# A fused mLSTM and feed-forward kernel: one list of steps in another order for the opening and the first 21 blocks, weight pieces without a maximum step, output gates in one run per partition

## The chip, the core and the metric

The kernel runs on one core of a Trainium2 chip. A core has a matmul engine (TensorE, here PE, with its weight loads shown apart as PEld), three engines for elementwise work (VectorE or DVE, ScalarE or ACT, GpSimd or POOL), and SyncE (SP), on whose queue this kernel puts all of its transfers. Each engine works through its own queue in order, and the engines wait for one another on semaphores. The metric is the device time of one execution in microseconds (us); lower is better.

## The reference

Four batches of 8 heads, 768 steps, head size 40, go through a gated recurrence with a running maximum m; the result, 3,072 tokens of 320 values, goes through a feed-forward layer with 2,048 hidden values.

```python
for t in range(S):
    m_new = np.maximum(f_gate[:, :, t] + m, i_gate[:, :, t])
    f_stab = np.exp(f_gate[:, :, t] + m - m_new)
    i_stab = np.exp(i_gate[:, :, t] - m_new)
    C = f_stab * C + i_stab * outer(vt, kt)
    n = f_stab * n + i_stab * kt
    h_tilde = C @ qt
    denom = np.maximum(np.abs(n @ qt), 1.0)
    y[:, :, t] = sigmoid(o_gate[:, :, t]) * h_tilde / denom
h = x @ w_in                     # x is y, as 3072 x 320
g = where(h >= 1, h, where(h <= -1, 0, (h + 1) ** 2 / 4))
out = g @ w_out
```

The weights come as 64-bit floats and are made into 32-bit ones in the kernel.

## The kernel before

The recurrence is cut into chunks of 128 steps: 6 chunks of 4 batches are 24 blocks n, four to a chunk. In a block the scores (k times q, one product per head) are multiplied by a matrix of decays and multiplied with the values; from the second chunk on, the state carried over the earlier chunks is added. Four blocks' results, turned, make one 512-token tile j of the feed-forward layer, which runs over 16 column blocks of 128: x = 16 j + block numbers them, 96 in all.

Every engine gets its instructions in the order of one list written out by hand, step by step; the class InOrder (line 102) keeps each engine to that order. There are two such lists. STEPS (line 37) is the opening: the gates' sums, the first four blocks, the first weight piece. ORDER (line 43) is all the rest. A step is a letter and a number. Those that matter here:

- loads on SP: Lg gates of chunk 0, Li the identity for transposes, Lq or Q the q/k tile of a block (two transfers of 160 KB), Lv2 values for two blocks, V values and keys of a block (from block 4 also q), P output gates of a chunk, L or Lw a weight piece (768 or 640 KB), A decays read back, Lf and Lc gates of chunks 1 to 4 and a mask
- PE: E in STEPS (Eb in the new list) the causal mask of a block's decays, A (Ab) the sums picked out of one tile, p (fs) a transpose of those sums, s or C scores, u or U product with the values, t or T the transposes of the result, K state product, I product with the carried state, M and N the two feed-forward products of a block x, J and j a score step with part of a feed-forward product
- elementwise: x or D the exponentials of the decays (ACT), m or c scores times decays (DVE), v or E values times gates (POOL), z s y (in STEPS r f y) the normalizer, the gate product and the result (DVE), x and w (in STEPS z) the high and low part of the turned result (ACT and DVE), Z the sigmoid of a chunk's output gates (ACT), R q r the hidden activation (ACT, ACT, DVE), B1 to B9 the gates of chunks 1 to 4 in a batch (B2 and B4 on DVE, B5 on POOL, B6 transposes on PE), k the state's mask
- the weight pieces: a digit 1 to 7 and the piece's place in the load order; 1 magnitude (ACT), 2 sign (DVE), 3 low half (POOL), 4 maximum (DVE), 5 the assembled word (DVE), 6 its high part (ACT), 7 its low part (DVE). Piece 0 is c, e and d in STEPS. Pieces go in turn to w_in and w_out; M needs a w_in piece for two blocks x, N a w_out piece. Raw pieces have two buffers (wraw)
- heating: wK in STEPS sets a count; the next PE step that calls hot() (line 495) first runs so many matmuls of zeros, 512 columns each, which no result uses

Product M of a block has eight matmuls of 512 columns: four with the high part of x, then two with its low part (made by w), then two more. From block x = 16 on the hidden values are split too (G and g).

load_og (line 510) fetches a chunk's output gates into the one buffer "sig". Its input has 1,280 bytes in a row for each step and batch. word_steps (line 411) and convert (line 437) make the weights.

Of the kernel before, what the change touches and what calls it, by code (L numbers as in the profile page):

```python
# [23 lines left out]
P = 128  # L24
# [12 lines left out]
STEPS = (  # L37
# [3 lines left out]
)  # L41
# [16 lines left out]
M24 u10 E11 A13 A12 r23 z10 G23 N21 R24 s10 y9 q24 y10 M25 r24 i11 G24 S13 g23 T9 R25 g24 N22 x9 S12 q25 w9 X9 D13.0
r25 K10 N23 k10 v11 V12 a10 G25 D12.0 g25 J11.26 N24 D12.1 c11.0 c11.1 U11 K11 u11 E12 N25 z11 V13 v12 k11 A14 s11 T10
p12 P3 M26 x10 y11 l12 D13.1 w10 X10 a11 T11 M27 x11 R26 w11 X11 q26 I12 R27 r26 I13 S14 q27 i12 M28.1 i13 G26 r27 e12  # L60
D14.0 g26 e13 j12.28 G27 M29 c12.0 Q13 R28 g27 Q14 q28 c12.1 Z3 N26 r28 m12 M30 b12 G28 N27 R29 g28 q29 K12 R30 r29
N28 v13 V14 q30 k12 G29 a12 M31 g29 r30 G30 N29 R31 g30 q31 M32 r31 G31 g31 I14 R32 M33 e14 q32 D14.1 r32 U12 G32 M34
# [36 lines left out]
TINY = 2.0  # L99
# [30 lines left out]
def mlstm_ffn_kernel(ctx, tc, qk, qn, vk, og, fi0, fi, fic, w_in, w_out, cst, out):  # L130
# [160 lines left out]
    def gate_exps(c):  # L291
        ex = exs.pop(c)
        tp = psum_a()[:, :P]
# [117 lines left out]
    def word_steps(k, w, raw, eng):  # L411
# [3 lines left out]
        if k > 1 and k != 4:  # L415
# [21 lines left out]
    def convert(k, nw, eng=nc.vector):  # L437
# [538 lines left out]
```

## Time and profile before

| | us |
|---|---|
| median of 3 runs | 486.82 |
| lowest and highest run | 486.24, 493.91 |
| span of the profiled execution | 496.1 |
| PE busy in it | 484.0 |
| DVE busy | 340.6 |
| ACT busy | 289.5 |
| POOL busy | 154.0 |

The profiled execution is one execution, with a span of its own. Its views show, for each engine, when each group of instructions began, how long it took, and what ended the idle time before it. PEclk is the granted clock of TensorE as a share of full speed: 1.00 is 2.4 GHz, 0.50 is 1.2 GHz.

### The profile page before, as it was taken

The numbers are of one execution on the slowest core, as the hardware profiler recorded it, in microseconds if no ns is written. First come the engines' busy times: TensorE is split into PE (matmuls) and PEld (weight loads), VectorE is DVE, ScalarE is ACT, GpSimd is POOL, SyncE is SP. The second block draws the span as 40 slices with busy tenths as digits, with TensorE's granted clock in tenths as the row PEclk, the third lists the DMA queues.
The fourth block names the chain that finished last, engine by engine and source line by source line (L and its number), as shares of the span: only waits on it lengthen the run. The fifth ranks groups of instructions, "written<-read, shape, count | busy, mean of one in ns | idle before, by whom it ended". The sixth has DMA issues, their size and how long they took to land.

```text
span 496.1 us, 8843 instructions
## 1 busy us (share of the span) xinstructions
PE 484.0 (98%) x3403; PEld 414.3 (84%) x3407; DVE 340.6 (69%) x598; ACT 289.5 (58%) x559; POOL 154.0 (31%) x175
## 2 busy tenths in 40 slices
PE   7998999999999999999998999999999999999997
PEld 3785787778779898989897988998989988988896
DVE  5548989899998968668667766948745577453332
ACT  4425786647756557674655954545765376275552
POOL 2503956564815514213324320313301142000000
PEclk8569899999999999999999999999999999999999
DMA  8935685754433215104433122202421100010001
GB/s 231 303 135 165 244 177 190 262 191 157 144 106 112 85 44 180 53 1 131 147 112 122 44 70 82 101 26 79 140 80 58 55 32 1 0 55 0 1 0 54
DMA packets 27737, 51.69 MB, mean 104 GB/s; under 512 B 8312, under 2 KB 17968, under 8 KB 27696
## 3 DMA queue, kind: packets, MB, share of 16 engines
q1 hardware_dynamic: 27696, 51.14, 32.2%
q8 instruction: 27, 0.44, 0.4%
q14 instruction: 14, 0.11, 0.1%
HBM read 47.09 MB, written 4.03 MB: 103 GB/s over the span
## 4 chain that ended last, share of the span: by engine, by line
PE 92%; DVE 3%; DMA 2%; ACT 1%; issue 1%; SPq 1%
PE pso L116 39%; PE psh L116 35%; PE psa L116 18%; DMA raw<-in_qk 1%; DMA qn<-in_qn 1%; DVE z L116 1%; ACT r L116 1%; SPq L116 0%; DVE wl L116 0%; DVE ow L116 0%; DVE sz L116 0%; DVE hv L116 0%; DVE r L116 0%; ACT sig L116 0%; DVE y L116 0%
## 5 line engine op out<-in xcount | busy, mean ns | idle before, releaser
L116 ACT ACTIVATE r<-psh,half 128x512 f32<-128x512 f32 x96 | 65.9, 687 | 90.5 <-PE psh L116 90.0
L116 PE MATMUL psh<-xh,wh 128*128 128x512 f32 x288 | 103.8, 415 | 1.2 <-DVE r L116 1.0
L116 DVE SCALAR_TENSOR_TENSOR r<-psh,r 128x512 f32<-128x512 f32 x96 | 65.8, 687 | 54.0 <-ACT r L116 53.2
L116 PE MATMUL pso<-oh,gh 128*128 128x320 f32 x320 | 101.9, 319 | 0.0
L116 PE MATMUL pso<-ow,gh 128*128 128x320 f32 x320 | 99.0, 309 | 0.0
L116 PE MATMUL pso<-oh,gl 128*128 128x320 f32 x320 | 98.9, 309 | 0.0
L116 PE MATMUL psh<-xh,wl 128*128 128x512 f32 (+1 forms) x274 | 94.7, 403 | 0.1
L116 DVE TENSOR_TENSOR gl<-r,gh 128x512 fp32r<-128x512 f32 x80 | 62.2, 786 | 27.7 <-ACT gh L116 27.5
L116 ACT CAST gh<-r 128x512 fp32r<-128x512 f32 x80 | 48.7, 617 | 46.5 <-DVE r L116 26.8
L116 PEld LDWEIGHTS pso<-oh,gh 128*128 128x128 f32 x320 | 60.2, 188 | 3.3 <-issue 0.7
L116 PEld LDWEIGHTS psh<-xh,wl 128*128 128x128 f32 (+1 forms) x274 | 51.6, 189 | 12.9 <-DVE wl L116 1.1
L116 ACT ACTIVATE r<-r 128x512 f32<-128x512 f32 x96 | 60.7, 632 | 2.7
L116 PEld LDWEIGHTS pso<-ow,gh 128*128 128x128 f32 x320 | 60.3, 188 | 1.9
L116 PE MATMUL psh<-xl,wh 128*128 128x512 f32 x192 | 61.0, 399 | 0.0
L116 PEld LDWEIGHTS pso<-oh,gl 128*128 128x128 f32 x320 | 60.1, 188 | 0.0
L116 PEld LDWEIGHTS psh<-xh,wh 128*128 128x128 f32 x288 | 49.2, 189 | 9.5 <-DVE r L116 1.5
L116 POOL TENSOR_TENSOR v<-vk,G 128x328 f32<-128x328 f32 x36 | 28.8, 801 | 80.1 <-PE psa L116 61.8
L116 ACT ACTIVATE Abc<-Abc,nA 128x128 f32<-128x128 f32 x160 | 50.1, 390 | 0.3 <-POOL Abc L116 0.2
L116 PEld LDWEIGHTS psh<-xl,wh 128*128 128x128 f32 x192 | 36.4, 190 | 8.8
L116 POOL TENSOR_TENSOR m<-m 128x1024 bf16<-128x1024 f32 x12 | 22.9, 1908 | 57.1 <-DVE m L116 57.1
L116 DVE TENSOR_TENSOR Abc<-psa,Abc 128x512 f32<-128x512 f32 x41 | 26.8, 685 | 18.1 <-PE psa L116 13.6
L116 PE MATMUL pso<-ow,r 128*128 128x320 f32 x128 | 37.6, 438 | 0.7 <-DVE ow L116 0.7
(178 smaller groups left out, 712.8 us busy)
## 6 DMA issues: line engine op xcount, KB each, us to landing
Abc<-a_d SPq DMA_DIRECT2D x20, 512.0 KB
raw<-in_qk SPq DMA_DIRECT2D x48, 160.0 KB
vk<-in_vk SPq DMA_DIRECT2D x20, 324.0 KB
wraw<-in_w_in SPq DMA_DIRECT2D x8, 768.0 KB
wraw<-in_w_out SPq DMA_DIRECT2D x8, 640.0 KB
sig<-in_og SPq DMA_DIRECT2D x6, 640.0 KB
qn<-in_qn SPq DMA_DIRECT2D x20, 180.0 KB
out<-o SPq DMA_DIRECT2D x22, 160.0 KB
```

The costliest lines, as they stand in the source:

```text
L116: r = getattr(self.engine, name)(*args, **kwargs)
```

## The change

STEPS and its loop go; the opening is the head of ORDER, with names of its own for what only the opening does (Lg, Li, Lf, Lc, Lv, Eb, Ab, fg, fs, ht, F). Four or fewer letters of a step can now be followed by "+K", the count of heating matmuls. The list is in another order up to step R24; behind that it is unchanged. Step 4 is gone from every weight piece, and step 1 scales by 2^-112 instead of 65,536, so that a zero stays zero. The output gates are laid out by the host as one run of 5,120 bytes per partition and chunk. The opening's block keeps the values' product in PSUM from values_mm itself. Two places more can run heating matmuls (gate_exps and batch_turn).

```diff
-STEPS = (
-    "Lg Li Lo Lq0 Lv0 Lq1 Lw0 Lq2 Lf Lv2 Lq3 Lw1 Lc o w9 E0 g0 q0 p A0 k0 x00 w2 s0 x01 m00 w1 E1 A1 h0 v0 x10 m01 "
-    "w2 s1 x11 v1 Lr0 Lr1 m10 c Lw2 w2 u0 m11 w2 E2 A2 x20 B0 w2 s2 r0 f0 y0 x21 v2 m20 m21 w2 u1 E3 A3 w1 t0 x30 e "
-    "w2 s3 v3 Lr2 Lr3 r1 f1 y1 x31 z0 m30 m31 w2 u2 t1 r2 f2 y2 w2 u3 z1 t2 r3 f3 y3 w8 z2 t3 W3 d z3 "
-)
 ORDER = """
-V4 Q4 Q5 P1 V5 M0 21 11 B1 22 Z1 41 M1 31 B2 B4 B5 51 L3 R0 B3 q0 61 r0 R1 71 32 B6 q1 M2 12 r1 v1 B7 42 L4 v0 52 K1
-v2 A4 R2 K0 A5 23 v4 A6 N0 q2 B8 k0 13 v3 r2 62 33 43 M3 k1 24 E4 L5 53 K2 34 R3 I4 k2 63 S4 N1 i4 q3 73 14 r3 S5 D4.1
...
+Lg fg1 fg2 P0 Z0 ht+7 L0 20 30 Li Eb0+7 fs Ab0 Eb1+3 D0.1 D0.0 10 Ab1 Q0 Lf Lv0 fg3 fg4 Q1 Lv2 E0 C0+1 Eb2+5 D1.0 B0
+50 D1.1 Ab2 D2.1 c0.0 Eb3+2 c0.1 C1 U0 c1.0 Ab3 c1.1 60 B1 z0 Q2 Q3 70 C2 E2 E1 D2.0 c2.0 D3.1 Q4 E3 B2 V0 s0 D3.0
+c2.1 U1 V1 z1 y0 s1 v1 C3+1 c3.1 U2+1 V2 c3.0 U3+3 y1 T0 z2 s2 z3 L1 T1+2 B3 y2 T2 v0 s3 y3 x0 x2 w0 K0 w2 x1 w1 T3 x3
+v2 w3 11 Lc K1 M0 V4 21 F R0 31 k0 B4 V3 B5 K2 k1 51 q0 M1 k2 61 v3 I4 L2 R1 r0 q1 71 22 32 r1 B6 A4 B7 i4 M2 12 52 M3
+K3 R2 L3 23 v4 k3 A5 R3 33 13 53 K4 q2 N0 L4 E4 63 q3 N1 r2 S4 D4.0 73 M4 D4.1 k4 r3 24 V5 M5 L5 14 C4 34 54 25 R5 V6
+15 35 B8 c4.1 P1 v5 55 R4 L6 S5 q4 r4 Q5 D5.1 N2 65 16 c4.0 75 26 L7 36 A6 D5.0 B9 q5 L8 N3 Z1 U4 u4 z4 L10 r5 t4 n4
...
-            nc.scalar.activation(w["mg"], hi.bitcast(F32), AF.Abs, scale=65536.0)
+            nc.scalar.activation(w["mg"], hi.bitcast(F32), AF.Abs, scale=2.0 ** -112)
...
-        elif k == 4:
-            eng.tensor_scalar_max(w["mg"], w["mg"], TINY)
...
-        nc.sync.dma_start(t, og.rearrange("(b c p) e -> c p b e", c=NC, p=P)[c])
+        nc.sync.dma_start(t.rearrange("p b e -> p (b e)"), og[c])
...
+    steps.update({
+        "Lg": first_gates, "Li": lambda: nc.sync.dma_start(ident, cst[:, :P]), "Lf": batch_loads,
+        "Lc": lambda: nc.sync.dma_start(cs_t, cst[0:120, P:]), "Lv": load_v2, "Eb": exponents, "Ab": add_sums,
+        "fg": first_gate_steps, "fs": first_sums, "ht": lambda: hot(psum_a()), "F": end_front,
+    })
     for what in ORDER.split():
-        steps[what[0]](*map(int, what[1:].split(".")))
+        what, _, n = what.partition("+")
+        heat = int(n or 0)
+        name = what.rstrip("0123456789.") or what[0]
+        steps[name](*map(int, filter(None, what[len(name):].split("."))))
...
-    a["og"] = nat(o_gate)
+    a["og"] = nat(o_gate).reshape(B, NC, P, DM).transpose(1, 2, 0, 3).reshape(NC, P, B * DM)
```

In the new list fg1 to fg4 are the first chunk's gates in four parts (running sums; their rests; the tail; a transpose on PE and the exponentials on ACT), and B0 is the batch's maxima, B in STEPS.

## Rows read from the trace of the kernel before

**Rows 1.** The page's busy time by engine: us, share of the span, instructions

```profile
PE 484.0 (98%) x3403; PEld 414.3 (84%) x3407; DVE 340.6 (69%) x598; ACT 289.5 (58%) x559; POOL 154.0 (31%) x175
```

**Rows 2.** Busy time by stretch: start:end, length, engines, PEclk, DMA share, GB/s

```profile
7.00:9.00 2.00, 0.65 (x5) 0.33 (x4) 1.21 (x6) 1.98 (x2) 0.39 (x2) 1.00 1.05 294
...
9.50:32.90 23.40, 22.71 (x123) 17.50 (x122) 10.53 (x21) 8.61 (x31) 6.47 (x10) 0.50 0.85 267
...
42.50:46.50 4.00, 3.99 (x16) 2.90 (x16) 3.87 (x10) 1.90 (x3) 1.70 (x2) 1.00 0.99 323
46.50:49.80 3.30, 0.89 (x5) 0.49 (x5) 1.59 (x3) 3.27 (x5) 2.99 (x6) 1.00 0.48 186
49.80:53.20 3.40, 3.30 (x7) 2.09 (x8) 3.22 (x4) 3.34 (x5) 3.20 (x4) 0.53 0.13 21
...
77.80:78.80 1.00, 0.26 (x2) 0.05 (x1) 1.00 (x2) 0.72 (x2) 0.36 (x2) 1.00 0.84 338
78.80:200.00 121.20, 121.20 (x853) 101.29 (x854) 106.30 (x176) 78.70 (x153) 59.52 (x60) 1.00 0.42 140
```

**Rows 3.** PE in time: start, us, operation, count, idle before and its releaser

```profile
8.96 2.04 PE L116 MATMUL pso<-raw 40*128 40x128 f32 x14 [0.74 <-DMA raw<-in_qk]
...
33.39 1.16 PE L116 MATMUL pso<-raw 40*128 40x128 f32 x16
34.48 0.39 PE L116 MATMUL pso<-zeros 128*128 128x512 bf16 x1
...
37.42 1.87 PE L116 MATMUL psa<-ow,A 128*128 128x41 f32 x16
39.12 0.53 PE L116 MATMUL psa<-ident,y 128*128 128x128 f32 x3
39.49 1.89 PE L116 MATMUL psh<-zeros 128*128 128x512 bf16 x8
...
42.50 0.71 PE L116 MATMUL psh<-xh,wh 128*128 128x512 f32 x2
...
47.64 0.33 PE L116 MATMUL psa<-ident,fi_s 128*128 128x128 f32 x1 [1.16 <-POOL fi_s L116]
49.01 0.33 PE L116 MATMUL psa<-ident,fi_s 128*128 128x128 f32 x1 [1.04 <-POOL fi_s L116]
...
58.82 0.79 PE L116 MATMUL psa<-ow 128*120 128x123 f32 x6
...
78.75 2.42 PE L116 MATMUL pso<-ow,r 128*128 128x320 f32 x8 [0.74 <-DVE ow L116]
```

**Rows 4.** The chain that ended last, 36 to 60 us: start, us, what

```profile
40.49 0.40 SPq L116
...
41.48 4.90 DMA qn<-in_qn
...
57.12 1.87 PE psh L116 x8
```

**Rows 5.** Busy time by stretch again, for the transfers at the start

```profile
0.00:5.00 5.00, 3.71 (x9) 1.34 (x10) 1.94 (x8) 1.28 (x1) 1.97 (x12) 1.00 0.57 150
...
0.00:10.00 10.00, 7.36 (x34) 3.52 (x36) 4.95 (x19) 4.56 (x6) 3.11 (x15) 0.95 0.79 214
```

**Rows 6.** Single rows in time of ACT, DVE and POOL, as in rows 3

```profile
13.68 2.17 ACT L116 ACTIVATE Abc<-pso,nA 128x128 f32<-128x128 f32 x8
...
40.91 0.41 DVE L116 TENSOR_TENSOR xl<-psa,xh 128x256 fp32r<-128x256 f32 x1
41.33 0.29 DVE L116 TENSOR_TENSOR xh<-psa,xh 64x128 fp32r<-64x128 f32 x1
...
46.57 1.02 POOL L116 TENSOR_TENSOR fi_s<-fi_s,ah_u 128x128 f32<-128x128 f32 x1 [1.95 <-DVE ah_u L116]
```

**Rows 7.** DVE by line and form, 40 to 200 us: busy, mean ns

```profile
L116 DVE TENSOR_SCALAR mg<-mg 128x640 f32<-128x640 f32 x8 | 6.7, 838 | 0.0
...
L116 DVE TENSOR_SCALAR mg<-mg 128x768 f32<-128x768 f32 x7 | 4.7, 664 | 0.0
```

More of the change, by code (lines that the diff above doesn't have):

```diff
@@ L58 @@
[L58 to L62, printed above, removed]
@@ new lines @@
+R14 214 M15 314 x7 S9 r12 q14 r13 514 N12 N13 i8 614 r14 w7 I9 72 215 K8 D9.1 M16 315 115 515 N14 i9 74 M17 X5 R15 X7
+76 p8 78 q15 r15 R16 a7 D8.0 612 C8 q16 k8 615 710 712 r16 N15 P2 c8.1 D10.1 M18.1 R17 c8.0 e9 O0.0 G16 O0.1 D10.0
+o0.1 q17 m8 b8 o0.0 J9.18 D9.0 g16 R18 l8 r17 G17 M19 Q10 U8 N16 c9.0 c9.1 O0.2 q18 r18 R19 e8 M20.1 O0.3 m9 b9 q19
+714 E9 j10.20 r19 u8 g17 G18 Z2 N17 Q12 p9 z8 l9 M21 R20 q20 c10.1 G19 v9 c10.0 A11 U9 s8 a8 v10 y8 K9 E10 M22 o0.2
+r20 o0.3 V11 I10 715 R21 q21 k9 u9 r21 T8 x8 G20 z9 g18 R22 Q11 M23 A12 N18 R23 g19 p10 l10 m10 G21 i10 w8 g20 q22 q23
@@ new lines @@
+r22 N19 G22 b10 a9 I11 e11 S11 e10 A13 U10 g22 N20 g21 E11 s9 r23 M24 u10 D11.1 D11.0 z10 N21 G23 X8 R24 s10 y9 q24
+y10 M25 r24 i11 G24 S13 g23 T9 R25 g24 N22 x9 S12 q25 w9 X9 D13.0 r25 K10 N23 k10 v11 V12 a10 G25 D12.0 g25 J11.26 N24
+D12.1 c11.0 c11.1 U11 K11 u11 E12 N25 z11 V13 v12 k11 A14 s11 T10 p12 P3 M26 x10 y11 l12 D13.1 w10 X10 a11 T11 M27 x11
+R26 w11 X11 q26 I12 R27 r26 I13 S14 q27 i12 M28.1 i13 G26 r27 e12 D14.0 g26 e13 j12.28 G27 M29 c12.0 Q13 R28 g27 Q14
+q28 c12.1 Z3 N26 r28 m12 M30 b12 G28 N27 R29 g28 q29 K12 R30 r29 N28 v13 V14 q30 k12 G29 a12 M31 g29 r30 G30 N29 R31
@@ new lines @@
+N38 u14 E15 G40 z14 G39 V17 D16.0 g40 J15.42 g39 M42 G41 s14 Q17 c15.1 A17 c15.0 N39 R42 g41 q42 y14 a15 U15 r42 T14
+u15 E16 A18 M43 x14 z15 S17 w14 X14 s15 I16 R43 y15 P4 M44 e16 q43 i16 D17.1 r43 p16 S18 T15 M45.1 x15 R44 w15 X15 l16
+q44 J16.45 R45 r44 q45 N40 c16.0 Q18 Z4 r45 c16.1 M46 m16 N41 b16 G43 G42 g43 M47 G44 g42 D18.0 g44 N42 R46 q46 U16
+R47 r46 q47 N43 u16 E17 A19 D18.1 r47 z16 M48 p17 G46 s16 l17 G47 g46 D17.0 N44 g47 S19 R48 M49.1 q48 G45 r48 D19.1
+g45 j17.49 M50 c17.0 Q20 R49 c17.1 q49 m17 N45 R50 q50 r49 b17 r50 K16 M51 k16 V18 v17 N46 R51 q51 r51 M52 G48 a16 g48
@@ new lines @@
+N47 R52 q52 M53 r52 O2.3 O2.1 o2.3 G49 o2.1 G51 g49 I17 M54.1 e17 g51 R53 i17 q53 O2.0 D19.0 J18.54 r53 o2.0 O2.2 M55
+H1 o2.2 Q19 c18.0 c18.1 N48 H2 H3 H4 U17 G50 y16 H5 g50 N49 E18 u17 R55 z17 R54 A21 I18 s17 q55 N50 i18 e18 G52 y17
+q54 g52 H6 T16 r54 K17 x16 H7 M56 v18 V19 k17 H8 S21 H9 w16 X16 N51 R56 H10 a17 q56 r55 K18 G54 H11 M57 G53 V20 k18
+v19 g54 g53 N52 H12 R57 r56 q57 I19 G56 r57 N53 e19 g56 i19 M58 N54 M59 G55 G57 g55 g57 R58 T17 H13 N55 x17 q58 w17
+X17 H14 r58 R59 K19 p18 N56 q59 m18 l18 D21.1 r59 b18 M60 G58 G59 g58 N57 R60 g59 q60 a18 D21.0 r60 U18 k19 N58 a19
@@ new lines @@
+E19 G60 u18 V21 g60 M61.1 A20 z18 s18 y18 j19.61 R61 q61 M62 c19.1 c19.0 r61 U19 R62 G61 S20 q62 g61 T18 A22 M63 x18
+r62 E21 D20.1 w18 X18 u19 N59 p21 R63 z19 l21 q63 s19 D20.0 I21 r63 P5 N60 S22 y19 G63 i21 D22.1 g63 C20 N61 c20.1 Q22
+G62 c20.0 Q23 D22.0 g62 T19 I20 x19 N62 i20 Z5 w19 X19 M64 N63 R64 q64 M65.1 O3.2 O3.1 r64 o3.1 o3.2 G64 j22.65 R65
+g64 q65 M66 c22.1 Q21 r65 O3.3 O3.0 M67 R66 c22.0 o3.0 o3.3 q66 G65 r66 N64 R67 g65 q67 G66 r67 J21.68 g66 G67 N65
+c21.1 c21.0 g67 M68 m21 N66 R68 b21 q68 r68 M69 G68 g68 N67 R69 q69 r69 M70 G69 g69 N68 R70 q70 r70 M71 G70 g70 N69
@@ new lines @@
+R71 q71 r71 U21 G71 N70 u21 E20 g71 V22 z21 M72 V23 p20 A23 s21 l20 m20 N71 R72 y21 q72 b20 r72 M73 G72 g72 U20 R73
+q73 M74 u20 E22 r73 z20 S23 G73 I22 R74 p22 T21 g73 l22 M75 x21 s20 q74 w21 X21 D23.0 y20 N72 i22 R75 m22 q75 T20 N73
+r74 b22 x20 r75 G74 w20 X20 G75 M76 g74 D23.1 g75 U22 R76 q76 M77.1 u22 E23 r76 z22 G76 j23.77 R77 g76 q77 s22 M78
+c23.1 c23.0 r77 N74 R78 y22 q78 r78 M79 G77 g77 I23 R79 T22 i23 q79 N75 x22 r79 w22 X22 U23 G78 g78 N76 u23 z23 s23
+N77 G79 y23 g79 T23 N78 x23 w23 X23 M80 N79 R80 q80 r80 M81 O4.1 O4.2 G80 o4.1 o4.2 g80 M82 R81 q81 r81 O4.3 R82 M83
@@ L92 @@
+o4.3 O4.0 G81 o4.0 q82 g81 N80 R83 r82 G82 q83 M84 g82 r83 G83 N81 R84 g83 q84 M85 r84 G84 g84 N82 R85 q85 r85 M86 G85
+g85 N83 R86 q86 r86 M87 G86 g86 N84 R87 q87 r87 M88 G87 g87 N85 R88 q88 r88 M89 G88 g88 N86 R89 q89 r89 M90 G89 g89
+N87 R90 q90 r90 M91 G90 g90 N88 R91 q91 r91 M92 G91 g91 N89 R92 q92 r92 M93 G92 g92 N90 R93 q93 r93 M94 G93 g93 N91
+R94 q94 r94 M95 G94 g94 N92 R95 q95 r95 N93 G95 g95 N94 N95 O5.0 o5.0 O5.1 o5.1 O5.2 o5.2 O5.3 o5.3
 """
@@ L292, in gate_exps @@
         ex = exs.pop(c)
-        tp = psum_a()[:, :P]
+        tp = psum_a()
+        hot(tp)
+        tp = tp[:, :P]
         nc.tensor.transpose(tp, ex, ident)
@@ L383, in batch_turn @@
         tp = batch["tp"] = psum_a()
+        hot(tp)
         for k, x in enumerate(batch["q"]):
@@ L409, in mlstm_ffn_kernel, with word_steps @@
     ol = {}
-    def word_steps(k, w, raw, eng):
+    def word_steps(k, w, raw):
         n = raw.shape[1] * raw.shape[2] // 2
         quarter = raw.rearrange("p k f -> p (k f)").bitcast(U16).rearrange("p (f w) -> p f w", w=4)
-        if k > 1 and k != 4:
+        if k > 1:
             out = w["out"].rearrange("p k f -> p (k f)").bitcast(I32)
@@ L435, in mlstm_ffn_kernel, with convert @@
     pieces = {}
-    def convert(k, nw, eng=nc.vector):
+    def convert(k, nw):
         kind, i = W_ORDER[nw]
@@ L449, in convert @@
         if k < 6:
-            word_steps(k, w, raws[kind, i], eng)
+            word_steps(k, w, raws[kind, i])
         elif k == 6:
@@ L687, in values_mm @@
                 nc.tensor.matmul(up[:, h * D1:(h + 1) * D1], t["A"][:, h, :], t["v1"][:, h, :], start=True, stop=True)
+        if n < B:
+            t["hv"] = up[:, :H * D1].rearrange("p (h d) -> p h d", d=D1)
     def values_add(n):
@@ L691, in values_add @@
         uv = t["up"][:, :H * D1].rearrange("p (h d) -> p h d", d=D1)
-        if n < B:
-            t["hv"] = uv
-        else:
-            nc.vector.tensor_tensor(out=t["hv"], in0=uv, in1=t["hv"], op=ALU.add)
+        nc.vector.tensor_tensor(out=t["hv"], in0=uv, in1=t["hv"], op=ALU.add)
     def normalizer(n):
@@ L816, in mlstm_ffn_kernel @@
     InOrder.on = True
-    for what in STEPS.split():
-        n = int(what[1]) if what[1:2].isdigit() else 0
-        hh = int(what[2:] or 0)
-        if what == "Lg":
-            first_gates()
-        elif what == "Lf":
-            batch_loads()
-        elif what[0] == "B":
-            batch_maxima()
-        elif what == "Lc":
-            nc.sync.dma_start(cs_t, cst[0:120, P:])
-        elif what == "Li":
-            nc.sync.dma_start(ident, cst[:, :P])
-        elif what == "Lo":
-            load_og(0)
-        elif what[:2] == "Lq":
-            load_qk(hh)
-        elif what[:2] == "Lv":
-            load_v2(hh)
-        elif what[:2] == "Lr":
-            load_v(hh)
-        elif what[:2] == "Lw":
-            load_w(*W_ORDER[hh])
-        elif what[0] == "s":
-            score_mm(n)
-        elif what[0] == "m":
-            score_mul(n, hh)
-        elif what[0] == "g":
-            sums = gate_sums(n)
-            for _ in range(4):
-                next(sums)
-        elif what[0] == "q":
-            run(sums)
-        elif what[0] == "k":
-            run(gate_tail(n))
-        elif what[0] == "h":
-            run(gate_exps(n))
-        elif what[0] == "A":
-            add_sums(n)
-        elif what[0] == "E":
-            exponents(n)
-        elif what[0] == "p":
-            first_sums()
-        elif what[0] == "v":
-            scale1(n)
-        elif what[0] == "o":
-            sigmoid(0)
-        elif what[0] == "x":
-            decay(n, hh)
-        elif what[0] == "c":
-            for k in range(1, 6):
-                convert(k, 0)
-        elif what[0] == "e":
-            convert(6, 0)
-        elif what[0] == "d":
-            convert(7, 0)
-        elif what[0] == "w":
-            heat = int(what[1:])
-        elif what[0] == "W":
-            heat = int(what[1:])
-            hot(psum_a())
-        else:
-            for f in dict(u=(values_mm, values_add), r=(normalizer,), f=(gate_out,), y=(finish_y,), t=(turn_y,),
-                          z=(x_high, x_low))[what[0]]:
-                f(n)
@@ L883, in mlstm_ffn_kernel, with end_front, first_gate_steps @@
-    front = False
-    gates.close()
-    mo = ctx.enter_context(tc.tile_pool(name="mo", bufs=2))
+    mo = None
+    def end_front():
+        nonlocal front, mo
+        front = False
+        gates.close()
+        mo = ctx.enter_context(tc.tile_pool(name="mo", bufs=2))
+    def first_gate_steps(k):
+        if k == 1:
+            batch["sums"] = gate_sums(0)
+            for _ in range(4):
+                next(batch["sums"])
+        elif k == 2:
+            run(batch["sums"])
+        elif k == 3:
+            run(gate_tail(0))
+        else:
+            run(gate_exps(0))
@@ L908, in mlstm_ffn_kernel @@
         "o": store, "H": last_gates, "B": lambda k: batches[k](),
-        "W": lambda w: convert(4, w, nc.gpsimd), "f": lambda n: state_add(n, nc.gpsimd),
+        "f": lambda n: state_add(n, nc.gpsimd),
         "t": lambda n: gate_out(n, nc.gpsimd), "n": lambda n: finish_y(n, nc.gpsimd),
     }
-    steps.update({str(k): (lambda w, k=k: convert(k, w)) for k in range(1, 8)})
+    steps.update({str(k): (lambda w, k=k: convert(k, w)) for k in (1, 2, 3, 5, 6, 7)})
+    steps.update({
[3 more added lines that the diff above has]
+    })
     for what in ORDER.split():
-        steps[what[0]](*map(int, what[1:].split(".")))
+        what, _, n = what.partition("+")
+        heat = int(n or 0)
+        name = what.rstrip("0123456789.") or what[0]
+        steps[name](*map(int, filter(None, what[len(name):].split("."))))
 _INS = ["qk", "qn", "vk", "og", "fi0", "fi", "fic", "w_in", "w_out", "cst"]
```

54 lines of the change are left out of this document (11 added, 43 removed).

## The prediction

> **What bounds the kernel now.** I read the busy shares first. PE is busy for 484.0 of 496.1 us [rows 1], so a gain has to come from PE's time: waits, stretches at half rate, or matmuls that do no work of the reference. DVE (340.6), ACT and POOL count only where PE waits for them.
>
> Then the table of busy time by stretch [rows 2]. Four stretches lose PE time. (a) From 9.5 to 32.9 us the granted clock is 0.50, the 1.2 GHz level, though PE is busy 22.71 of 23.40 us; ahead of the fall, from 7 to 9 us, PE did 0.65 us of work in 2.0. (b) From 46.5 to 49.8 PE works 0.89 of 3.30 us, and then (c) from 49.8 to 53.2 the clock is 0.53 once more. (d) From 77.8 to 78.8 PE works 0.26 us. From there to 200 us PE is busy 121.20 of 121.20 us, and soon the part of the list begins that both kernels share.
>
> Third, PE's order of instructions [rows 3]: what each kind costs at either level, and that the first block's matmuls on the w_in weights (M0) begin at 42.50. Everything ahead of them is the opening, everything behind is one long queue on PE. So the total is: start of M0, plus the work behind it, plus the waits behind it.
>
> Fourth, the chain of waits behind M0 [rows 4]. The load of the second chunk's output gates (P1) sits on SP right behind two other loads in the list and reuses the one buffer that the first chunk's last gate product reads. It is issued at 40.49 when that product is done; the transfers behind it land at 46.38, and only then can ACT run the sigmoid (Z1) at the head of its queue. Behind Z1 stand R0, the square, and the cast of the second weight piece (step 6 of piece 1), for which PE waits until 49.8. In the same gap PE waits 1.16 and 1.04 us for POOL's fi_s, which is B5's result and which B6 transposes [rows 3].
>
> **The profiled execution and the runs.** Its span is 496.1 us, 9.3 above the median of 486.82. Stretch (a) at full rate would be 22.71 / 2 = 11.4 shorter, so I put the 9.3 there: I take the median execution as one without most of (a), with M0 at 42.5 - 9.3 = 33.2 us. Halving alone would give 31.1; the 2.1 between them are waits that the slow clock covers. The sum is made as span 496.1, less 9.3 for (a), less the terms below.
>
> **The steps are the same steps.** Counted by kind, the new list has every step of the two old ones, but for the 16 maximum steps and 8 heating matmuls (40 before, 32 now). From step R24 on, the lists agree word for word. So real PE work does not change, and only its place does.
>
> **Opening, transfers.** SP issues the gates (128 KB), then the output gates P0 (640), the first weight piece L0 (768), the identity Li (64) and only then the first q/k tile Q0 (320). Before, the tile stood behind 832 KB and its last half released PE at 8.96 [rows 3]. DMA moved 0.75 MB by 5 us and 2.14 MB by 10 us, 278 GB/s between [rows 5]. Q0's last byte was number 1.15 M, at 5 + 0.40 / 0.278 = 6.4 us by that rate, so landing lags the count by up to 2.5 us. Now it is number 1.92 M: 9.2 us by count, 10.2 to 11.7 with a lag of 1.0 to 2.5. The identity is number 1.60 M, 8.1 us by count, 9 with a lag of 1. The sums of the first gates (fs) wait for it; behind fs on PE's queue stand the eight pick matmuls, the next block's mask and its picks, the transposes of fg4, and C0. On DVE, 20 (piece 0) is ahead of fs's own instruction and of fg3's five subtractions, so fg3 ends about 11.2. I take C0 at 11.5 us. That is 2.5 later than before; in return mask, picks and transposes of the second block, which before came behind the scores, are done. P0's longer packets (5,120 instead of 1,280 bytes) may bring the sigmoid's input up to 1 us sooner; ACT then waits for nA from fs anyway, so I count nothing, and at worst nothing.
>
> **Opening, PE from C0 to M0, at 2.4 GHz**, from starts of neighbouring rows [rows 3]: four score sets at 1.09 (33.39 to 34.48) are 4.36; four value products at 1.70 (37.42 to 39.12) are 6.80; four transposes at 0.37 are 1.48; two masks and two pick sets, each of two times 512 columns like two heating matmuls, are 1.72; 15 heating matmuls at 0.215 (eight took 1.89 with the last one's drain) are 3.23; K0 and K1, which now stand here, 0.63 each (0.79 in the row, less some 0.16 of drain that the next matmul covers, as between 37.42 + 1.87 and 39.12), 1.26. Sum 18.9, so M0 at about 30.5. ACT keeps up: eight sets of four exponentials at about 1.09 (eight took 2.17 [rows 6]) with steps 10 and 60 in between, begun near 9.7, end near 21, just as C3 needs the buffer they read. DVE is late at the end: y3 comes at about 29.4, four w steps of 0.7 follow (0.41 + 0.29 [rows 6]), so w3 ends at 32.2, while M0 needs it after its first four products at 31.4: a wait of 0.8. Before, M0 and M1 took the 4.0 us from 42.5 to 46.5 [rows 2] where a block's eight products take 1.87 [rows 4], so they lost 0.25.
> Term 1: M0 begins at 30.5 against 31.1 by the same way of reckoning: -0.6. Term 2: K0 and K1 are already done: -1.3. Term 3: the wait at w3: 0.8 - 0.25 = +0.5.
>
> **Behind M1.** P1 now stands behind B8, and Z1 behind N3, far from any wait. ACT goes straight on to R0, the square and step 61, and SP is no longer held by P1. (b) cost 3.30 - 0.89 = 2.41 us and (c) 3.30 x (1 - 0.53) = 1.55. What is late next: PE does M0 until 33.2, K2, M1 and I4, and comes to B6 at 36.3. B6 needs B5, which took POOL 2.5 us (46.57 to 49.0 [rows 3, 6]) and needs B4; that stands on DVE behind w3, 21 and k0, so it ends near 34.4, and B5 at 36.9. M2 wants the low part of piece 1 (71) at 37.7; on DVE k1, 51, k2 and r0 stand before it, and it ends near 38.3. Together 1.2 us of waits, of which some may lie in one another: 1.0, between nothing and 2. Term 4: 1.0 - 2.41 - 1.55 = -3.0.
>
> **The maximum step.** It is 8 x 0.838 + 7 x 0.664 us [rows 7] and one more for piece 0, 12 us of DVE. Nearly all of it lies beside a busy PE, so it counts only in (d), where PE waited 0.74 for the out-piece [rows 3]: the maximum of that piece (about 0.8) and the wait are of one size. Term 5: -0.7, at best; at worst nothing. The new scale, 2^-112 for 65,536, leaves the same ACT instruction: nothing.
>
> Sum: 496.1 - 9.3 - 0.6 - 1.3 + 0.5 - 3.0 - 0.7 = **481.7**.
>
> **The rule on the clock.** The trace shows half rate over 23.4 us with PE busy 97% of it [rows 2]. The Trainium skill ("TensorE: Matmul & The Clock Gate", Part 1) says that half rate is the default, that sustained activity releases it, and that idling brings it back, at points that vary from run to run. It speaks against this change, which has fewer heating matmuls. [...]
>
> **Rivals.**
> *The clock falls in the new opening* (the other side). Place: the wait for the identity, from about 7 us (14 heating matmuls and the mask end there) to 9, or the score and value products from 15 to 23 us, where the new list has 1 heating matmul where the old had 2 before nearly every step. For: from 7 to 9 us PE had little to do in the trace, and the clock fell. Against: here three heating matmuls, a mask and two pick sets follow at once. Price: a stretch like (a), 9.3, so 481.7 + 9.3 = **491.0**; up to 11.4 by halving, or 18.9 if all from C0 to M0 ran at half, 500. It decides if the granted clock shows 0.50 for over 12 us before M0; under 10 us of it the kernel is still not slower than before.
> *The gain is given back to the weights.* PE comes 3 us sooner to M2 with four small products more done, and steps 23 and 53 stand on DVE right behind the load L3, which cannot be issued before POOL's 31 has freed its buffer (about 33); a load at this place took 4.9 us [rows 4], so it lands near 38, and DVE comes to 23 at about 41.4. Against: 3.4 us of slack, and 12 us less on DVE. Should it land 6 us later, M4 waits 3 to 4: **485**.
> *More is gained.* The 2.1 us of waits between 31.1 and 33.2 go too, Q0 lands 1.3 sooner and the 1.0 behind M1 vanishes: 481.7 - 4.4 = **477.3**.
> *The step list is no gain at all* (the opening as long as before, other waits in place of (b)): 486 to 487, counted with the second rival.
>
> **Chances.** The forecast (478.5 to 484.5): 0.56. Clock (486 to 497): 0.20. Gain given back or none (484.5 to 487.5): 0.13. More gained (475 to 478.5): 0.11. The time forecast is 481.7, the likeliest case's. Leaving out half of the last and the upper half of the clock's cases gives 477 to 490.5. About 2% is what a measurement of this kernel can tell from no change: faster than 477.1 needs most of the fourth case, 0.09; slower than 496.6 needs the clock's case with its long stretch, 0.06; within 2%, 0.85.
>
> **What would show it.** Term 1 and 2: M0 begins at 29 to 32 us at clock 1.00 with two psa<-ow state products ahead of it; C0 between 10.2 and 11.7. Term 3: a PE wait of under 1 us for DVE's xl inside M0. Term 4: no wait on the sigmoid, no fall of the clock near 45 us, waits for POOL's fi_s under 0.5. Term 5: no wait for an out-piece on DVE. The forecast is wrong if the clock is 0.50 in the opening, if PE waits for wraw or win beyond 40 us, or if C0 begins behind 13.

## The result, and the profile after

| | before | after |
|---|---|---|
| median in the first comparison, us | 488.25 (4 runs) | 479.45 (4 runs, 478.95 to 479.97) |
| ratio, with 95% interval | | 0.9837 [0.9812, 0.9863] |
| span of the profiled execution | 496.1 | 477.7 |
| mean granted clock in it | 0.972 | 1.00 |

The change makes the kernel 1.6% faster, 7 to 9 us; the forecast was 481.7 in a range of 477.0 to 490.5. A run's time stands 1.7 to 2.1 us above the span of the same execution (here 479.5 against 477.7), so the execution shown of the kernel before took about 498 us, well above the median: its clock was at half rate in the opening. The experiments below therefore begin with the kernel before once more.

The kernel after, first the page's busy time by engine (us, share of the span, instructions):

```profile
PE 468.7 (98%) x3399; PEld 404.6 (85%) x3399; DVE 322.5 (68%) x582; ACT 286.5 (60%) x559; POOL 154.3 (32%) x175
```

The same kernel, busy time by stretch as in [rows 2] (start:end, length, PE, PEld, DVE, ACT, POOL, granted clock, DMA share, GB/s). The stretches end at the first scores (C0), at M0, at M2, and beyond:

```profile
0.00:10.80 10.80, 7.84 (x40) 3.53 (x40) 6.20 (x21) 5.00 (x8) 4.49 (x16) 1.00 0.82 271
10.80:30.60 19.80, 19.53 (x187) 16.36 (x187) 15.78 (x37) 11.19 (x36) 9.55 (x14) 1.00 0.86 285
30.60:36.95 6.35, 5.93 (x33) 4.71 (x33) 6.18 (x13) 3.29 (x6) 2.75 (x5) 1.00 0.46 167
36.95:50.00 13.05, 13.05 (x63) 10.14 (x61) 10.22 (x15) 9.11 (x21) 11.81 (x11) 1.00 0.78 270
```

The granted clock is 1.00 throughout, PE is packed from C0 to M0 (19.53 of 19.80 us), and the gap behind M1 with the fall of the clock behind it [rows 2] is not there. PE in time, as in [rows 3]:

```profile
7.82 0.21 PE L111 MATMUL pso<-ident,ac 32*128 32x32 f32 x1 [1.44 <-DMA ident<-in_cst]
...
10.36 0.30 PE L111 MATMUL pso<-ident,ex 128*128 128x128 f32 x1 [0.23 <-DVE ex L111]
...
10.80 1.16 PE L111 MATMUL psa<-raw 40*128 40x128 f32 x16
...
30.62 0.71 PE L111 MATMUL psh<-xh,wh 128*128 128x512 f32 x2 [0.29 <-DVE xh L111]
...
36.64 0.33 PE L111 MATMUL psa<-ident,fi_s 128*128 128x128 f32 x1 [0.40 <-POOL fi_s L111]
...
36.95 0.71 PE L111 MATMUL psh<-xh,wh 128*128 128x512 f32 x2
```

The identity arrives late and holds PE for 1.44 us; C0 begins at 10.80, M0 at 30.62, M2 at 36.95. Between M1 and M2 only B6 waits, 0.40 us for POOL.

### The profile page after: what moved, and what is told of

Its sections match the earlier page's. It is cut to its first block, busy times and chain, and to the rows that moved or that the text cites. A ratio compares the mean times of both kernels' runs of the same rounds, so it can differ in the third digit from the quotient of the medians.

```text
span 477.7 us, 8809 instructions
## 1 busy us (share of the span) xinstructions
PE 468.7 (98%) x3399; PEld 404.6 (85%) x3399; DVE 322.5 (68%) x582; ACT 286.5 (60%) x559; POOL 154.3 (32%) x175
## 4 chain that ended last, share of the span: by engine, by line
PE 91%; DVE 6%; DMA 1%; issue 1%; POOL 1%; ACT 0%; SPq 0%; DVEq 0%; POOLq 0%
PE pso L111 38%; PE psh L111 37%; PE psa L111 16%; DMA ident<-in_cst 1%; DVE win L111 1%; DVE C L111 1%; DVE z L111 1%; POOL fi_s L111 1%; DVE xl L111 0%; DVE y L111 0%; DVE r L111 0%; DVE xh L111 0%; DVE sz L111 0%; DVE hv L111 0%; ACT r L111 0%
## 5 line engine op out<-in xcount | busy, mean ns | idle before, releaser
L111 POOL TENSOR_TENSOR m<-m 128x1024 bf16<-128x1024 f32 x12 | 24.2, 2017 | 60.4 <-DVE m L111 50.7
L111 DVE TENSOR_TENSOR Abc<-psa,Abc 128x512 f32<-128x512 f32 x43 | 28.1, 684 | 15.6 <-PE psa L111 15.3
```

What stands on the lines that cost most here:

```text
L111: r = getattr(self.engine, name)(*args, **kwargs)
```

## The experiments

All ratios are to the kernel before on the same chip, with 95% intervals. Runs that are compared with the changed kernel stand beside its own second measurement (a_again: 479.36 us, 5 runs from 478.80 to 479.90, ratio 0.9829 [0.9813, 0.9845]).

### The kernel before once more

> The kernel before, unchanged, for its clock and span in several executions. If the 496.1 us of the profiled execution came from the half-rate stretch between 9.5 and 32.9 us, then executions with a mean clock near 1.00 take 484 to 487 us, and those with a stretch at 0.50 in the opening 8 to 12 us more. If the stretch cost nothing, the times would not follow the mean clock.

Measured: 488.35 us (10 runs, 486.14 to 489.76). The profiled execution (span 487.6, 489.49 us, the second longest of the ten) kept its clock in the opening. Its busy time by stretch:

```profile
9.50:31.20 21.70, 21.40 (x184) 15.83 (x182) 18.30 (x40) 12.39 (x41) 7.16 (x10) 1.00 0.88 285
31.20:35.00 3.80, 3.75 (x16) 2.93 (x16) 3.67 (x9) 0.56 (x1) 1.70 (x2) 1.00 0.97 321
35.00:40.50 5.50, 1.11 (x6) 0.45 (x4) 1.91 (x4) 4.58 (x6) 4.73 (x9) 0.96 0.39 142
40.50:45.00 4.50, 4.14 (x10) 2.87 (x11) 3.86 (x5) 4.02 (x8) 1.48 (x3) 0.50 0.28 80
45.00:50.00 5.00, 5.00 (x24) 4.23 (x24) 2.73 (x5) 2.74 (x4) 4.68 (x6) 0.81 0.93 367
```

PE in time, the same execution:

```profile
31.25 0.70 PE L116 MATMUL psh<-xh,wh 128*128 128x512 f32 x2
...
36.52 0.33 PE L116 MATMUL psa<-ident,fi_s 128*128 128x128 f32 x1 [1.28 <-POOL fi_s L116]
37.89 0.33 PE L116 MATMUL psa<-ident,fi_s 128*128 128x128 f32 x1 [1.04 <-POOL fi_s L116]
...
40.55 1.19 PE L116 MATMUL psh<-xh,wh 128*128 128x512 f32 x2 [2.12 <-DVE r L116]
```

M0 begins at 31.25: halving stretch (a) of [rows 2] gives 31.1, to 0.15 us. But M2 begins 9.3 us after M0 where it was 7.3 in the execution with the slow opening (42.50 [rows 3] to 49.79). The gap costs 5.50 - 1.11 = 4.4 us instead of 2.4, and the clock falls behind it: 0.50 from 40.5 to 45 and 0.81 to 50, which is 4.14 x 0.5 + 5.00 x 0.19 = 3.0 us of PE's time.

B6's two waits for POOL are nearly the same in both executions (1.28 and 1.04 here, 1.16 and 1.04 there). The difference is M2's wait, 2.12 us here and 0.23 there, at the end of the chain that begins with the second chunk's output gates. Their load was issued 1.9 us ahead of M0 here (29.35) and 2.0 there (40.49 [rows 4]), but ACT's table load for the sigmoid, which needs them, begins 6.5 us after the issue here and 4.6 there, where the view names DVE for its wait, so that the gates were there by then. M2 and that table load in the execution shown of before, then the table load here:

```profile
49.79 1.01 PE L116 MATMUL psh<-xh,wh 128*128 128x512 f32 x2 [0.23 <-DVE r L116]
```

```profile
45.11 1.28 ACT L116 ACT_TABLE_LOAD   x1 [2.09 <-DVE ow L116]
```

```profile
35.88 1.28 ACT L116 ACT_TABLE_LOAD   x1 [4.12 <-DMA sig<-in_og]
```

So the gap differs from execution to execution with the landing of one transfer. The next run shows that a quick opening alone does not make it longer. Why the transfer took longer here was not seen.

Over the executions the mean clock was 0.991 to 0.996, and those at 0.991 to 0.993 took 487.9 to 489.8 where those at 0.995 and 0.996 began at 486.1. So the time does follow the clock, but in the profile it is the clock behind M1. A long fall in the opening, as in the execution shown of before, is rare at most: one of the 31 runs of before on this chip had a mean clock below 0.99, with 493.0 us, and where its clock fell was not seen.

### Heating through the thin stretch before the first scores

```diff
-... k0 x00 w2 s0 x01 ...
+... k0 x00 w8 s0 x01 ...
```

> The kernel before with 8 heating matmuls instead of 2 ahead of the first scores (s0), so that PE works through the stretch from 7 to 9 us in which it waited for the first q/k tile. If that thin stretch brought the clock down, the granted clock stays 1.00 up to M0 in every execution, M0 begins near 31 us, and the median is 486, against 488 for the kernel before. The rival, that the score and value products themselves are too thin to hold the clock, gives a fall behind 9.5 us all the same and 490 or more in some executions.

Measured: 487.01 us, ratio 0.9989 [0.9964, 1.0013]. PE was busy for 2.00 us from 7 to 9, M0 began at 30.90, and the clock still fell behind the gap (0.62 from 38.7 to 43.0). M0 and M2, then the gap and the stretch behind it:

```profile
30.90 0.70 PE L116 MATMUL psh<-xh,wh 128*128 128x512 f32 x2
...
38.72 1.19 PE L116 MATMUL psh<-xh,wh 128*128 128x512 f32 x2 [0.64 <-DVE r L116]
```

```profile
34.60:38.70 4.10, 1.15 (x6) 0.47 (x5) 1.98 (x4) 4.06 (x6) 3.30 (x7) 0.98 0.52 189
38.70:43.00 4.30, 4.29 (x16) 3.36 (x17) 3.90 (x5) 4.24 (x9) 3.70 (x4) 0.62 0.27 81
```

Here the opening is as quick as in b_again, but the sigmoid's table load begins 5.0 us after the issue of the gates' load, and M2 7.8 us after M0. The gap costs 4.10 - 1.15 = 2.95 us and the fall 4.29 x 0.38 = 1.6, close to the execution with the slow opening.

The median shows no difference: on this chip the opening of the kernel before hardly ever lost its clock anyway, so this run can't tell what brought it down in the execution shown of before.

### P1 and Z1 moved in the kernel before

```diff
-V4 Q4 Q5 P1 V5 M0 21 11 B1 22 Z1 41 M1 ...
+V4 Q4 Q5 V5 M0 21 11 B1 22 41 M1 ... D5.0 c4.1 P1 L7 ... 65 M5 Z1 u4 ...
```

> The kernel before with P1 behind c4.1 and Z1 behind M5, so that neither SP nor ACT waits for the second chunk's output gates behind M0. By the prediction's chain this wait carries stretch (b): 2.4 us less, 4 with stretch (c), 482 to 484. But in the trace POOL's fi_s released PE at 49.0, only 0.8 before the cast of piece 1 did, so two chains end together there; if that is right, moving one of them alone gives 0.5 to 1 us, 485 to 486.

Measured: 486.33 us, ratio 0.9968 [0.9943, 0.9994]; 1.6 us by the ratio, not 4. One of the ten executions, at a mean clock of 0.972 as in the execution shown of before, took 497.8 us; it was not profiled and is not in the ratio. ACT ran R0 at 33.07 instead of 38.35 in b_again. PE in time, waits behind M1:

```profile
36.12 0.33 PE L116 MATMUL psa<-ident,fi_s 128*128 128x128 f32 x1 [1.27 <-POOL fi_s L116]
38.09 0.47 PE L116 MATMUL psa<-ident,fi_s 128*128 128x128 f32 x1 [1.64 <-POOL fi_s L116]
```

The wait of M2 for DVE's r (2.12 in b_again) is gone, but B6's second wait for POOL grew from 1.04 to 1.64, and the clock fell all the same (0.83 mean from 32 to 42 us). Two chains end in that gap. Moving one of them leaves the other.

### P1 and Z1 moved back in the changed kernel

```diff
-w3 11 Lc K1 M0 V4 21 F R0 31 ...
+w3 11 Lc K1 M0 V4 P1 21 Z1 F R0 31 ...
```

(P1 and Z1 are taken out at their new places.)

> The changed kernel with P1 put back right behind V4 and Z1 right behind step 21, ahead of R0, as the old list had them. ACT would then wait for the output gates' transfer, issued near 28.5 us behind the last gate product and landing some 5 us later, and run the sigmoid for 1.3 us before R0: M2 some 2 us later, 481 to 482, and if the clock falls there again, 483. If the place of P1 and Z1 is worth nothing: 479.5.

Measured: 481.14 us beside 479.36 for a_again (ratios 0.9864 [0.9843, 0.9885] and 0.9829 [0.9813, 0.9845], whose intervals just touch): 1.8 us between the medians, as expected. ACT in time, in the one profiled execution:

```profile
32.70 1.28 ACT L111 ACT_TABLE_LOAD   x1 [1.78 <-DMA sig<-in_og]
33.99 1.28 ACT L111 ACTIVATE sig<-sig 128x1280 f32<-128x1280 f32 x1
35.17 0.67 ACT L111 ACTIVATE r<-psh,half 128x512 f32<-128x512 f32 x1
```

The table load waits 1.78 us for the output gates, and R0 begins at 35.17 instead of 33.04. M2 then waits only 0.27 us for r and 0.19 for wl, and M0 to M2 is 6.85 us against 6.33. This execution is the shortest of the four (479.46 us) and lost nothing in sum against the changed kernel's own profile: N0 begins 1.15 us later (43.25 against 42.10), block 24 only 0.7 later (152.87 against 152.18). The three others took 481.0 to 481.9 us and were not profiled, so where they lose some 2 us is not shown.

### The maximum step: taken out of the old list, put back into the new

```diff
 before, without it:
-            eng.tensor_scalar_max(w["mg"], w["mg"], TINY)
+            pass
 after, with it:
+        elif k == 4:
+            nc.vector.tensor_scalar_max(w["mg"], w["mg"], 2.0)
-... 50 ... 51 ...
+... 40 50 ... 41 51 ...
```

(Each has the scale of step 1 that goes with it.)

> The kernel before with the maximum step left out and the scale 2^-112. By the prediction 0.7 us for stretch (d), and up to 0.5 more because one maximum stands on DVE ahead of B2 and B4: 485 to 486. If DVE's 12 us were the true cause of the change's gain, it would give 5 us or more: 481 or less.

> The changed kernel with the maximum step back in all 16 pieces (right ahead of step 5, scale 65,536). By the prediction DVE's 12 us lie beside a busy PE: 0 to 1 us more than the changed kernel, 479.5 to 480.5. If the freed DVE time is a real part of the gain: 3 us or more, 482.5.

Measured: 485.77 us, ratio 0.9959 [0.9937, 0.9981], for the old list without the step; 484.16 us, ratio 0.9937 [0.9920, 0.9953], for the new list with it, which is 4.8 us above a_again. The first agrees with the expectation (1.6 us), the second does not. The kernel after and a_max, the same stretches (two rows each):

```profile
38.00:60.00 22.00, 22.00 (x121) 17.12 (x121) 15.96 (x25) 17.65 (x36) 13.35 (x11) 1.00 0.79 250
60.00:101.00 41.00, 40.87 (x246) 32.86 (x244) 32.44 (x57) 29.16 (x56) 27.64 (x28) 1.00 0.72 224
```

```profile
38.00:60.00 22.00, 21.06 (x108) 15.55 (x107) 20.22 (x26) 16.06 (x36) 12.51 (x12) 1.00 0.73 252
60.00:101.00 41.00, 39.29 (x239) 31.41 (x239) 37.19 (x62) 28.48 (x52) 24.91 (x26) 1.00 0.72 211
```

From 38 to 101 us DVE goes from 48.4 to 57.4 us of 63, and PE loses 0.94 + 1.71 us by waiting. In a_max PE's waits from 38 to 101 us, by what ended them (total, times, longest):

```profile
PE psh L112 <- DVE r L112: 1.6, 2, 1.2
PE psh L112 <- DVE wl L112: 0.6, 1, 0.6
PE psa L112 <- DVE C L112: 0.5, 1, 0.5
```

All of them name DVE; the kernel after has no such wait in that stretch. From M0 to block 24 PE took 125.73 us in a_max and 121.56 in the kernel after: 4.2 us. The other 1.1 us of the profiled execution lie ahead of M0, where the identity landed later (a wait of 2.66 instead of 1.44), before any maximum runs, so they are not the step's. The list of a_max was ordered for weights without the step, and each maximum stands right ahead of step 5; another place for it was not tried, so the 4.2 us are its price in this order.

The parts alone and together, in ratios: order, heating and layout without the removal 0.9937; the removal without the order 0.9959; both 0.9829. Alone they give 0.63% and 0.41%, together 1.71%. The new order hands PE its work sooner, and DVE has the time for it only without the maximum.

### The heating matmuls behind the start

```diff
-... Eb1+3 ... C0+1 Eb2+5 ... Eb3+2 ... C3+1 ... U2+1 ... U3+3 ... T1+2 ...
+... Eb1 ... C0 Eb2 ... Eb3 ... C3 ... U2 ... U3 ... T1 ...
```

> The changed kernel with only the 14 heating matmuls at the start; the 18 others are left out. They take PE 3.9 us. If PE's queue alone sets M0 and the clock holds without them, M0 begins 2 to 3 us sooner: 477. If the clock falls without them: 5 to 12 us more, 485 to 491. If they fill waits for ACT, DVE and transfers: no change, 479.5.

Measured: 486.49 us, ratio 0.9950 [0.9918, 0.9982]; 7.1 us more than a_again by the medians, 5.9 by the ratios. Nine of ten executions had a mean clock of 0.969 to 0.979 and took 485.4 to 489.5; one, at 0.989, took 479.7. Busy time by stretch in a profiled execution with the fall (M0 at 39.44):

```profile
10.40:15.00 4.60, 3.39 (x35) 2.27 (x36) 3.44 (x4) 4.60 (x19) 2.14 (x3) 1.00 0.69 230
15.00:20.00 5.00, 5.00 (x40) 4.68 (x38) 2.09 (x6) 2.53 (x9) 3.55 (x7) 0.63 1.05 291
20.00:39.40 19.40, 19.40 (x104) 18.53 (x105) 11.73 (x30) 4.32 (x13) 3.95 (x5) 0.50 0.47 168
```

The 18 matmuls cost 3.9 us of PE and are worth 6 to 7 net: without them the clock falls between 15 and 20 us, during the score and value products, and stays at 0.50 up to M0 with PE busy all of the time. This is the prediction's clock rival, at its second place, at 6 to 10 us where 9.3 was forecast. What brought the clock down is not settled by it: from 10.4 to 15 us PE also waited 1.2 of 4.6 us, most of it for ACT's exponentials, where in the changed kernel it is busy 4.60 of 4.60. A run with the heating matmuls gone and that wait filled in another way was not made.

### The layout of the output gates

```diff
-        nc.sync.dma_start(t.rearrange("p b e -> p (b e)"), og[c])
+        nc.sync.dma_start(t, og.rearrange("(b c p) e -> c p b e", c=NC, p=P)[c])
```

> The changed kernel with the output gates in their old layout (1,280 bytes in a row). The prediction counts nothing for it. Since the first chunk's gates now go ahead of the first weight piece and the identity, a slower transfer also makes these late, and PE waited 1.44 us for the identity: at most 1 us, 479.4 to 480.4. If the layout carried a real part of the gain: 482 or more.

Measured: 479.79 us, ratio 0.9836 [0.9817, 0.9855], beside 0.9829 for a_again on another chip. No difference that these runs can show.

### Three versions of the first 10 us

```diff
 a_li:
-Lg fg1 fg2 P0 Z0 ht+7 L0 20 30 Li Eb0+7 fs Ab0 Eb1+3 D0.1 D0.0 10 Ab1 Q0 Lf Lv0 fg3 fg4 ...
+Lg Li fg1 fg2 P0 Z0 ht+7 L0 Eb0+7 fs Ab0 Eb1+3 D0.1 D0.0 10 Ab1 Q0 Lf Lv0 fg3 20 30 fg4 ...
 a_li_q:
+Lg Li fg1 fg2 Q0 P0 Z0 ht+7 L0 Eb0+7 fs Ab0 Eb1+3 D0.1 D0.0 10 Ab1 Lf Lv0 fg3 20 30 fg4 ...
 a_tail:
+Lg Li fg1 fg2 fg3 P0 Z0 ht+7 L0 Eb0+7 fs Ab0 Eb1+3 D0.1 D0.0 10 Ab1 20 30 Q0 Lf Lv0 fg4 ...
+        if c == 0:
+            nc.scalar.activation(spare, half, AF.Exp)
```

> The changed kernel with the identity's load (Li) right behind the first gates' and steps 20 and 30 behind fg3, so that neither the identity nor the first weight piece holds the first gates' tail. PE's wait of 1.44 us goes, nA is there near 6.6 instead of 8.1, and C0 begins when the first q/k tile has landed, 9.5 to 10.5 instead of 10.8 to 11.1. PE is packed from C0 to M0, so M0 and the end come 0.5 to 1.5 us sooner: 478 to 479. If ACT or the second q/k tile sets the pace instead: no change, 479.4.

> As the run before, and the first q/k tile's load (Q0) right ahead of the output gates', so that it lands some 4 us sooner. C0 then follows the transposes of fg4 near 9.0: 1.5 to 2 us less than the changed kernel, 477.5 to 478. But the sigmoid and the first weight piece come 1 us later on ACT and DVE; if one of them is on the path: no better than the run before.

> The changed kernel with Li right behind the first gates' load, fg3 ahead of fs on DVE, steps 20 and 30 behind Ab1, and one exponential of a 128x1 tile right behind the first sigmoid, so that ACT's table load (1.28 us, at 8.3 in the changed kernel, behind its wait for nA) is done before nA is there. The run a_li moved the first gates' tail alone and gained 0.4 us, within its spread, because ACT's exponentials still began at 9.5. Here they begin near 8.5 and the transposes of fg4 wait for nothing: C0 near 10.3, M0 0.6 to 1 us sooner, 478.2 to 478.8. If a thinner PE near 8 to 10 us brings the clock down, as in a_li_q: 486 to 490. If neither ACT nor the tail sets the pace: 479.4.

Measured: a_li 478.99 us, ratio 0.9820 [0.9801, 0.9840]; a_tail 478.88, 0.9817 [0.9791, 0.9843]; a_again 479.36, 0.9829 [0.9813, 0.9845]. Both may be some 0.5 us better, but the intervals overlap almost wholly, so no version is shown to beat the changed kernel. a_li_q took 488.57 us: five of its six executions had a mean clock of 0.975 to 0.978 and took 488.4 to 490.3, one at 1.00 took 479.5. Its profile is of that one; where the clock falls in the others was not seen.

PE in time in a_li, the wait of a_li's transposes, and then the same place in a_tail:

```profile
4.25 3.06 PE L111 MATMUL psh<-zeros 128*128 128x512 bf16 x7
...
10.49 0.30 PE L111 MATMUL pso<-ident,ex 128*128 128x128 f32 x1 [0.47 <-DVE ex L111]
```

```profile
9.60 0.48 PE L111 MATMUL psa<-raw 40*128 40x128 f32 x2
10.72 1.13 PE L111 MATMUL psa<-raw 40*128 40x128 f32 x14 [0.64 <-DMA raw<-in_qk]
```

In a_li the second seven heating matmuls took 3.06 us instead of 1.69, because full rate came later in that execution, so the identity was no longer what PE waited for and the rest came no sooner (C0 at 10.94, M0 at 30.83). In a_tail the scores begin at 9.60, wait 0.64 us for the second half of the first q/k tile, and M0 comes at 30.55 instead of 30.62. An earlier C0 is lost again on the way to M0: in a_li_q's profile they stand at 10.17 and 31.00. Identity, first gates' tail, ACT's exponentials and the tile all arrive within about a microsecond of one another.

## Why the prediction was right, and where its terms were off

- **The profiled execution and the runs.** The step took 9.3 us as the difference between a span (496.1) and a run's time (486.82). Span to span it is 11.0 to 11.4, as much as halving (a) gives. So M0 of a usual execution is not at 33.2 us: b_again has it at 31.25, b_heat at 30.90. The 2.1 us that the step called hidden waits are, but for some tenths, the 1.7 to 2.1 us by which a run's time exceeds its span. The sum was not harmed, since it thereby starts at the median run.
- **The chain behind M0.** What landed at 46.38 is the qn transfer [rows 4]. The sigmoid ran at 46.41 because its table load had begun at 45.11 and takes 1.28 us, so the output gates were there by 45.11.
- **Opening, transfers.** C0 was taken at 11.5, with 10.2 to 11.7 as bounds; it came at 10.80, and at 9.6 to 11.9 in the other kernels with the new list. The identity was put at about 9 us and released PE at 7.8; what held C0 in the profile was the tail fg3, as the prediction's chain had it, 0.23 us at the last step.
- **Terms 1 to 3.** M0 at 30.62, forecast 30.5; 31.25 before, forecast 31.1: the gain of 0.6 is there to 0.1 us. That is partly luck: C0 came 0.7 us sooner than taken, and from C0 to M0 PE took 19.8 us instead of 18.9. K0 and K1 run at 28.54 and 29.54, ahead of M0, as term 2 says. The wait at w3 was forecast at 0.8, inside M0. In the trace M0 waits 0.29 at its start for xh, no wait is listed inside it, and it takes 2.17 us (30.62 to 32.79) where a packed block takes 1.87 [rows 4].
- **Term 4** named the right place and both chains, and was mis-sized. The new waits were put at 1.0; they are 0.40 for B6 and nothing for M2. The old cost, 2.41 + 1.55, is that of one execution; it is 2.95 + 1.6 in b_heat and 4.4 + 3.0 in b_again. So the term is worth -3.6, -4.2 or -7.0 by the execution one starts from, where -3.0 was forecast. The two runs on it show why no single step carries it: moving P1 and Z1 alone gave 1.6 us in the old list, where B5's chain ends in the same gap, and moving them back cost 1.8 us in the new one.
- **Term 5** is too small in both lists. In the old one 0.7 was forecast at best and 1.6 measured, with an interval of 0.9 to 3.1; in the new one the maximum would cost 4.8 us. The failed step is "nearly all of it lies beside a busy PE": that was read from the old order, in which PE waited elsewhere. The view of the kernel before could have warned: DVE was busy 106.30 of the 121.20 us behind stretch (d) [rows 2].
- **The rivals.** The clock did not fall in the changed kernel: 0.998 to 1.00 in all of its runs. The clock rival is real all the same: taking 18 heating matmuls away brings it about at its second place, for 6 to 7 us, and with the first tile's load brought forward (a_li_q) five of six executions took 9 us more at a lower mean clock, at a place that was not seen. The gain was not given back to the weights: in the changed kernel's profile PE waited neither for a raw piece nor for win. "More is gained" did not come to 477.3.
- **The sum.** 481.7 against 479.45: 2.3 us too high. Behind M0 the kernels can be compared at the start of block 24, up to which PE has the same steps behind it in both lists. It begins, in the execution shown of before, b_again, b_heat, a_max and the kernel after, at

```profile
170.44 0.71 PE L116 MATMUL psh<-xh,wh 128*128 128x512 f32 x2
...
162.75 0.71 PE L116 MATMUL psh<-xh,wh 128*128 128x512 f32 x2
...
159.07 0.71 PE L116 MATMUL psh<-xh,wh 128*128 128x512 f32 x2
...
157.47 0.63 PE L112 MATMUL psh<-xh,wh 128*128 128x512 f32 x2
...
152.18 0.63 PE L111 MATMUL psh<-xh,wh 128*128 128x512 f32 x2
```

which is 127.9, 131.5, 128.2, 125.7 and 121.6 us after M0 (at 42.50, 31.25, 30.90, 31.74 and 30.62). Terms 2 to 5 add up to 4.5 us less than in the execution shown of before; it is 6.4 less. Some 0.9 of the missing 1.9 are waits put in and not met, 0.6 behind M1 and 0.3 in M0; the rest was not traced to steps. The total is also nearer than its split. Without the removal the new list gains 0.63%, 3.1 us, where terms 1 to 4 add up to 4.4, and the removal then adds 4.8 to 5.3 where the sum had 0.7. One side was too large and the other too small, and that they partly cancel is luck.

The rule of the Trainium skill that the prediction weighed ("TensorE: Matmul & The Clock Gate", Part 1: half rate is the default, sustained activity releases it) is contradicted once more by a_start_heat, where PE was busy 19.40 of 19.40 us at 0.50. That the point of change varies from run to run agrees: the same seven heating matmuls took 1.69 us in one kernel's execution and 3.06 in another's.

## What to carry to other kernels

A stall read from one profiled execution is one sample: with the fall of the clock behind it, the same gap cost 4.0, 4.6 and 7.4 us in three profiles of the same order of steps, and the difference began with the landing of one transfer. A span is to be compared with a span and a run's time with a run's time. A step on an engine that is hidden beside the bottleneck has a price that belongs to the order, so a change that lets the bottleneck run earlier and a change that frees the helper engine should be measured together as well as apart. Where two chains end in one gap, moving one of them buys only the distance to the other.

## What the runs showed of the hardware

- PE can be busy 100% of a stretch of 19 us with the granted clock at 0.50 (a_start_heat, 20 to 39.4 us), with score products of 40 rows, value products of 41 columns, transposes, state products and their weight loads. With 18 matmuls of zeros among them, 3.9 us of PE's time, the changed kernel's clock stayed at 1.00. Such matmuls did not end a fall, though: at least ten of them lie in the stretch at 0.50 of the execution shown of before (9.5 to 32.9 us [rows 2]).
- A shift of one load by two places (a_li_q against a_li) moved the mean granted clock from 1.00 in all four executions to 0.975 to 0.978 in five of six. Where in the execution it fell was not profiled.
- At the start the clock's row reads 1.00 while the heating matmuls of 512 columns follow one another at the half-rate pace: eight in 3.62 us in the execution shown of before, against seven in 1.69 us in the kernel after once full rate had come. The rate of the first microseconds is read from the matmuls, not from that row. The two rows:

```profile
1.69 3.62 PE L116 MATMUL psa<-zeros 128*128 128x512 bf16 x8
...
4.25 1.69 PE L111 MATMUL psh<-zeros 128*128 128x512 bf16 x7
```

- The same transfer of 640 KB was there at the latest 4.6 us after its issue in one execution of the kernel before (40.49 to 45.11), and 6.5 us after it in another (29.35 to 35.88).
